# A spectral filter and a snake MLP on one core: the w_in load, batch 1's x loads, its first and inverse pieces and a negation are moved

## The chip, the core and the metric

The kernel runs on one core of one Trainium2 chip. The metric is device time in microseconds of a whole execution; lower is better. Three executions of the kernel before gave 787.63, 787.67 and 788.89 us, a median of 787.67.

## What is computed

```python
x: 8 x 3008 x 256 f32; filt_r, filt_i: 1505 x 256; w_in: 256 x 2048; w_out: 2048 x 256; alpha: 2048
X = rfft(x, axis=1)                       # over the 3008 tokens, per channel
y = irfft(X * (filt_r + 1j*filt_i))       # a circular filter, per channel
h = y.reshape(24064, 256) @ w_in
g = h + sin(alpha*h)**2 / alpha           # "snake"
out = g @ w_out                           # 24064 x 256 f32
```

## The kernel before, in words

**The filter.** The transform of 3008 = 47 x 64 points is done with matmuls in f16 in four kinds of piece, for each batch b, in class Spectral. *first* (L178, matmul L181, result pa): the DFT over 47, 16 pieces of 94x512; four of them fill a quarter of t_h, which SP stores to DRAM (d<-t_h, L186). *load_t2* (L193): eight DMAs issued by POOL bring that back transposed (t<-d); all of them read every quarter. *forward* (L201, result pb): the DFT over 64 with its twiddles, 12 pieces; ACT evacuates pb to xf (L204), and SP swaps xf's halves into xs with two DMAs (L208). *product* (L215) and *cross* (L221, L222) multiply by the filter on DVE, the cross with xs. *inverse* (L232, result pc), 12 pieces; three of them fill g, which SP stores (d<-g, L239). *load_t4* (L244) reads that back (t_a<-d), and *last* (L254, result pd), 16 pieces, gives y, with channels on partitions. Evacuations of pa, pc and pd go through `evac` (L160 on ACT, L162 on DVE), every third on DVE by a counter that runs over the program. pa, pb, pc and pd of all batches share two PSUM buffers (pool fps).

Batch 0 has a way of its own without DRAM: transposes on DVE (L413), matmuls L399, L431, L453, products L441, and L343 for the last step, whose later parts are put between other matmuls one by one ("between").

**The MLP.** 48 chunks of up to 512 columns of y. *hidden* (L540, ph, two matmuls of 512 columns; cos on ACT, L544; L545 on DVE makes v), 16 per chunk, with four PSUM buffers. *project* (L557, po, eight matmuls of 256 columns; copy to o, L565; stores, L585, half a dozen small DMAs on SP for 256 rows).

**Start-up.** POOL's queue loads x of batch 0, the table d_t, the filter and the table e_t. The filter comes in four quarters (L303), two halves g of the frequencies, real (k = 0) and imaginary (k = 1), each in two DMAs; `marks["filt", g, k]` is the second DMA of a quarter. The first of SP's six w_in loads (L468) waits for one of these marks; SP's queue is in order, so the other w_in loads, two small tables (L471, L472) and the two halves of w_out (L475) come after it. weights_in (L482) multiplies w_in by alpha on POOL, in six products, the first after batch 0's last filter product; weights_out (L514) multiplies w_out by -0.5/alpha on POOL in three, and on ACT (L512) for the last four blocks. Between these products POOL issues batch 1's four x loads (L141), of which each needs w_out's first half to have landed. w_out's buffer is the one that v of chunk 1 takes.

**The order.** It is written by hand: a chunk has 8 steps, and each step records two hidden, then what is due, then project, then what is due half a step later (loop at the end). `put(at, ...)` gives a piece its due step; `slot` takes pieces that are due in that order, but only one PE piece at a time unless the next is more than a step late. Each engine executes its instructions in the order recorded. For batch 1: first at 7.9 + 0.3 i, load_t2 at 12.5, inverse at 23.5 + 1.25 u, forward 6 steps before its inverse, product half a step and cross four steps after forward. negate (L602) turns the sign of one half of the imaginary filter, after batch 0 is done with it, in two instructions on DVE at 13 and 14.

The lines most used below are 141, 160, 162, 181, 193, 201, 204, 208, 221, 222, 232, 239, 244, 254, 343, 468, 482, 514, 540, 544, 545, 557, 565, 585 and 602.

Of the kernel before, what the change touches and what calls it, by code (L numbers as in the profile page):

```python
# [62 lines left out]
def kernel(  # L63
# [10 lines left out]
    nc = tc.nc  # L74
# [12 lines left out]
    def after(ins, other):  # L87

        tc.add_manual_dep(ins.ins, other.ins.name, mybir.DependencyInfo(
            mybir.DependencyClass.Sync, mybir.DependencyReason.DATA), reason="order of loads")  # L90
# [43 lines left out]
    f_t = [filt_t[:, k] for k in range(2)]  # L134

    marks = {}
# [150 lines left out]
    def spread_alpha(i):  # L287

        ps = hps.tile([128, 4, 128], FP32, name=f"al_bc_{i}", tag="h")
        for a in range(4):  # L290
            for k, part in enumerate(parts):
                nc.tensor.matmul(out=ps[:, a, :], lhsT=one[:, 4 * i + a:4 * i + a + 1].to_broadcast([128, 128]),
                                 rhs=part, start=(k == 0), stop=(k == 2))
        nc.scalar.copy(out=alpha[:, i // 2, 512 * (i % 2):512 * (i % 2) + 512], in_=ps.rearrange("p a b -> p (a b)"))

    for g in range(2):
        gs = slice(12 * g, 12 * g + 12)
        for k, filt in enumerate((filt_r, filt_i)):
            for q in range(2):
                if (g, k, q) == (0, 1, 1):  # L300
                    split_alpha()
                off, step = ((12 * g) * C, C) if q == 0 else ((N1 - 12 * g) * C, -C)
                marks["filt", g, k] = nc.gpsimd.dma_start(  # L303
                    out=f_t[k][64 * k + 32 * q:64 * k + 32 * q + 32, gs, :],
# [158 lines left out]
    for g in range(6):  # L463
        own, tag = (t2pool, "t2") if g < 3 else (gpool, "g")
        j0 = 1024 * (g // 3) + 384 * (g % 3)
        js = slice(j0, j0 + (256 if g % 3 == 2 else 384))
        w_in32.append((js, own.tile([128, 2, js.stop - js.start], FP32, name=f"w_in_{g}", tag=tag)))
        ins = nc.sync.dma_start(out=w_in32[g][1], in_=w_in_v[:, :, js])  # L468
        if g == 0:
            after(ins, marks["filt", 1, 1])  # L470
    nc.sync.dma_start(out=wf_t, in_=wf_dram.ap())  # L471
    nc.sync.dma_start(out=wi_t, in_=wi_dram.ap())  # L472
    w_out32 = vpool.tile([128, 16, C], FP32, name="w_out32", tag="v")
    for jb in range(0, 16, 8):
        ins = nc.sync.dma_start(out=w_out32[:, jb:jb + 8],  # L475
                                in_=moe_w_out[128 * jb:128 * jb + 1024].rearrange("(b p) c -> p b c", p=128))
        marks.setdefault("w_out", ins)
    s1 = Spectral(1)
# [37 lines left out]

    spread_alpha(2)
    spread_alpha(3)
    for step in ([(weights_in, g) for g in range(6)] + [(s1.load_x, 0), (weights_out, 0), (s1.load_x, 1),
                 (weights_out, 4), (s1.load_x, 2), (weights_out, 8), (s1.load_x, 3)]):  # L520
        step[0](*step[1:])
    warm_pe(12)
    last_0(0, 4)
# [69 lines left out]
    def put(at, fn, *args, pe=False):  # L593
        pending.append((at, len(pending), pe, fn, args))
# [4 lines left out]
    def negate(i):  # L599

        gs = slice(12 * i, 12 * i + 12)
        nc.vector.tensor_scalar(out=f_t[1][0:64, gs, :], in0=f_t[1][0:64, gs, :],  # L602
                                scalar1=-1.0, scalar2=None, op0=ALU.mult)

    for i in range(2):
        put(13 + i, negate, i)
    for n0, n, at in ((6, 5, 1.5), (11, 4, 12.5), (15, 4, 14), (19, 4, 15.5), (23, 4, 17), (27, 5, 19)):
        put(at, last_0, n0, n, fps, "f", True)
    for b in range(1, B):
        s = s1 if b == 1 else Spectral(b)  # L610
        z = 48 * b
        if b > 1:
            for ch in range(4):
                put((22,27,32,37)[ch] if b == 2 else z - 92 + 7 * ch, s.load_x, ch)
        for i in range(16):
            put(7.9 + 0.3 * i if b == 1 else 36 + 0.66 * i if b == 2 else z - 67 + 0.66 * i, s.first, i, pe=True)
        for g in range(4):
            put(12.5 if b == 1 else max(z - 56, 46.5), s.load_t2, g)
        for u in range(12):
            inv = 23.5 + 1.25 * u if b == 1 else 59 + 2.1 * u if b == 2 else z - 40.8 + 2.3 * u  # L620
            fwd = inv - (6 if b == 1 else 6)
            put(fwd, s.forward, u, pe=True)
            put(fwd + (0.5 if b == 1 else 1.5), s.product, u)
            if s.fused:
                put(fwd + (4 if b == 1 else 4.5), s.cross, u)
            put(inv, s.inverse, u, pe=True)
        for ch in range(4):
            put(z - (9.5 if b == 1 and ch < 3 else (10.5, 10.5, 10.5, 3)[ch]), s.load_t4, ch)
        for u in range(16):
            put(z + (u - (5 if b == 1 else 6.5) if u < 4 else 2 * u - 9), s.last, u, pe=True)  # L630
# [15 lines left out]
    step = 0  # L646
# [43 lines left out]
```

## Time and profile before

| | us |
|---|---|
| median of three runs | 787.67 |
| span of the profiled execution, first to last instruction | 786.7 |
| PE busy from 36 to 48 (of 12 us) | 11.28 |
| 48 to 64 (16) | 14.55 |
| 64 to 72 (8) | 6.76 |
| 72 to 80 (8) | 7.81 |
| 80 to 100 (20) | 20.00 |
| 100 to 118 (18) | 17.12 |
| 118 to 135 (17) | 16.96 |
| 135 to 200 (65) | 64.87 |

The profile is of one execution. No time of its own is listed for it beside its span; the span is 1.0 us under the median of the runs, which also holds what lies before the first instruction and after the last. Busy time of PE counts a matmul until its modelled end, and matmuls are pipelined, so a stretch that is busy throughout can still hold waits: what PE loses is better read from the starts of its matmuls. The granted clock is full in all 40 slices of the span. In the lines quoted below, "0.67 <-ACT t_h L160" at the end of a line is the idle time of the engine before it and what ended that; "x4" is the number of instructions merged; a matmul's own 0.38 us is its latency, not its share of the engine's time.

### The profile page before, as it was taken

How to read it: one execution, taken by the hardware profiler on the slowest of the kernel's cores; microseconds unless marked ns; L12 is line 12 of the kernel's file. 1: busy time of each engine (PE TensorE's matmuls, PEld its weight loads, DVE VectorE, ACT ScalarE, POOL GpSimd, SP SyncE). 2: the span in 40 equal slices, each digit the busy share in tenths (PEclk: the TensorE clock that was granted, in tenths of full speed). 3: DMA queues.
4: the chain of work that ended last, by engine and by line, in shares of the span. 5: the costliest groups of instructions: out<-in, count | busy, mean ns of one | idle time of the engine just before them, and what ended most of it. 6: DMA issues, size and time to landing. Idle time of an engine off the chain costs nothing.

```text
span 786.7 us, 16619 instructions
## 1 busy us (share of the span) xinstructions
PE 773.5 (98%) x5799; PEld 535.0 (68%) x5799; DVE 657.6 (84%) x1172; ACT 616.5 (78%) x1208; POOL 79.5 (10%) x125
## 2 busy tenths in 40 slices
PE   8998999999999999999999999999999999999998
PEld 4756766666667766777666766777666776766666
DVE  7887997899878997799977998799987999777773
ACT  5797878888878887888877888788887887777674
POOL 6442000200020000200020000200002000000000
PEclk9999999999999999999999999999999999999999
DMA  9965568665473646554575454845556243421111
GB/s 213 258 131 157 113 145 223 153 123 133 134 198 84 134 99 195 143 120 110 120 200 128 103 106 139 224 87 113 129 155 181 61 99 81 117 62 28 41 41 54
DMA packets 87692, 100.99 MB, mean 128 GB/s; under 512 B 14488, under 2 KB 75944, under 8 KB 87608
## 3 DMA queue, kind: packets, MB, share of 16 engines
q1 hardware_dynamic: 78032, 73.73, 34.5%
q0 software_dynamic: 9360, 26.15, 17.7%
q8 instruction: 45, 0.74, 0.4%
q14 instruction: 39, 0.32, 0.1%
q10 hardware_dynamic: 216, 0.05, 0.0%
HBM read 55.72 MB, written 46.66 MB: 130 GB/s over the span
## 4 chain that ended last, share of the span: by engine, by line
PE 89%; DVE 5%; ACT 2%; DMA 2%; issue 1%; SPq 1%; ACTq 0%; DVEq 0%
PE po L557 39%; PE ph L540 38%; PE pa L181 3%; PE pd L254 2%; DVE v L545 2%; PE pb L201 2%; PE pc L232 2%; DMA xs<-xf 1%; ACT cos_all L544 1%; DMA al<-in_moe_alpha_dram 1%; PE warm L381 1%; PE pc L453 0%; SPq L585 0%; ACT t_h L160 0%; DVE filt_t L162 0%
## 5 line engine op out<-in xcount | busy, mean ns | idle before, releaser
L545 DVE SCALAR_TENSOR_TENSOR v<-cos_all,ph 128x512 f16<-128x512 f32 (+1 forms) x768 | 483.0, 672 | 108.1 <-ACT cos_all L544 104.8
L544 ACT ACTIVATE cos_all<-ph 128x512 f32<-128x512 f32 (+1 forms) x768 | 411.1, 592 | 93.9 <-PE ph L540 92.9
L540 PE MATMUL ph<-y,w 128*128 128x512 f16 (+1 forms) x1536 | 388.4, 374 | 1.7 <-DVE y L162 0.9
L557 PE MATMUL po<-w,v 128*128 128x256 f16 x3008 | 389.5, 272 | 0.0
L557 PEld LDWEIGHTS <-v 128*128 128x128 f16 x3008 | 288.3, 98 | 77.7 <-issue 1.4
L540 PEld LDWEIGHTS <-w 128*128 128x128 f16 x1536 | 147.9, 98 | 106.5 <-issue 6.1
L565 ACT COPY o<-po 128x512 f32<-128x512 f32 (+1 forms) x97 | 55.6, 574 | 20.2 <-PE po L557 12.9
L204 ACT CAST xf<-pb 128x512 f16<-128x512 f32 x84 | 50.0, 595 | 16.4 <-PE pb L201 12.7
L193 POOL DMA_DIRECT2D t<-d x56 | 36.4, 669 | 204.6 <-DMA out_dram<-o 99.8
L160 ACT CAST t_h<-pa 96x512 f16<-96x512 f32 x74 | 43.3, 585 | 10.6 <-PE pa L181 10.5
L141 POOL DMA_DIRECT2D x<-in_x_dram x32 | 17.1, 536 | 298.2 <-PE pc L232 171.2
L160 ACT CAST y<-pd 128x376 f16<-128x376 f32 (+1 forms) x82 | 39.5, 482 | 8.8 <-PE pd L254 5.3
L254 PEld LDWEIGHTS <-t_a 96*128 96x128 f16 x448 | 31.3, 97 | 18.7 <-issue 0.4
L181 PE MATMUL pa<-x,wf_t 94*96 94x512 f16 x112 | 42.3, 381 | 1.6 <-ACT t_h L160 1.3
L160 ACT CAST g<-pc 128x512 f16<-128x512 f32 x58 | 34.4, 593 | 8.0 <-PE pc L232 7.7
L222 DVE TENSOR_TENSOR p<-p,xs 128x512 f16<-128x512 f16 x84 | 35.7, 425 | 2.9
L254 PE MATMUL pd<-wi_t,t_a 96*128 96x94 f16 x448 | 37.1, 204 | 0.0
L221 DVE TENSOR_TENSOR xs<-xs,filt_t 128x512 f16<-128x512 f16 x84 | 35.2, 420 | 0.8 <-DMA xs<-xf 0.8
L215 DVE TENSOR_TENSOR p<-xf,filt_t 128x512 f16<-128x512 f16 x84 | 35.2, 419 | 0.0
L232 PE MATMUL pc<-p,e_t 128*128 128x256 f16 x168 | 32.1, 273 | 0.8 <-ACT xf L204 0.5
L201 PE MATMUL pb<-t,d_t 128*128 128x256 f16 x168 | 32.1, 272 | 0.2
L162 DVE CAST y<-pd 128x376 f16<-128x376 f32 (+2 forms) x46 | 24.9, 544 | 1.5 <-PE pd L343 1.0
(66 smaller groups left out, 264.4 us busy)
## 6 DMA issues: line engine op xcount, KB each, us to landing
x<-in_x_dram POOLq DMA_DIRECT2D x30, 376.0 KB, 4.9
d<-t_h SPq DMA_DIRECT2D x28, 384.0 KB
t<-d POOLq DMA_DIRECT2D x56, 192.0 KB, 4.6
xs<-xf SPq DMA_DIRECT2D x168, 64.0 KB
d<-g SPq DMA_DIRECT2D x56, 192.0 KB
t_a<-d SPq DMA_DIRECT2D x28, 384.0 KB
out_dram<-o SPq DMA_DIRECT2D x104, 80.0 KB
w_out<-in_moe_w_out_dram SPq DMA_DIRECT2D x2, 1024.0 KB
```

The source lines that it names most:

```text
L160: marks["act"] = nc.scalar.copy(out=dst, in_=src)
L181: marks["pe"] = nc.tensor.matmul(out=ps[0:NK, :], lhsT=wf_t, rhs=self.x[ch][:, 2 * j:2 * j + 2, :], start=True, stop=True)
L193: nc.gpsimd.dma_start(out=self.t2[g][64 * p:64 * p + 64, :, :], in_=self.d1[a0:a0 + 6, :, :].rearrange("s n c -> n s c"))
L201: nc.tensor.matmul(out=ps[:, i, :], lhsT=d_t[:, s, :], rhs=self.t2[s // 6][:, s % 6, :], start=True, stop=True)
L204: nc.scalar.copy(out=self.xf[u], in_=ps)
L232: nc.tensor.matmul(out=ps[:, i, :], lhsT=e_t[:, 2 * w + i, :], rhs=pt[:, i, :], start=(k == 0), stop=(k == len(pr) - 1))
L254: nc.tensor.matmul(out=psv[:, i, :], rhs=wi_t, start=True, stop=True, lhsT=t4_h[ch // 2][0:NK, n0 % 16 + i, cb * 128:cb * 128 + 128])
L540: nc.tensor.matmul(out=ps[:, 0:n], lhsT=w1[:, cb, jb * 128:jb * 128 + 128], rhs=y_cols[:, cb, c0:c0 + n], start=(cb == 0), stop=(cb == 1))
L544: nc.scalar.activation(out=cs[:, 0:n], in_=ps[:, 0:n], func=AFT.Sin, bias=float(np.pi / 2))
L545: marks["snake"] = nc.vector.scalar_tensor_tensor(out=v[k][:, jb, 0:n], in0=cs[:, 0:n], scalar=-1.0, in1=ps[:, 0:n], op0=ALU.add, op1=ALU. ...
L557: nc.tensor.matmul(out=pso[k][:, t % 2, :], lhsT=v[k][:, jb, 128 * t:128 * t + 128], rhs=w2[:, jb, :], start=(jb == 0), stop=(jb == 15))
L565: nc.scalar.copy(out=o[:, i0:t % 2 + 1, :], in_=pso[k][:, i0:t % 2 + 1, :])
```

## The change

w_in's first load waits for the second half's real quarter, the third of four, in place of its imaginary quarter, the last. POOL issues batch 1's x loads between the last w_in products, and all w_out products come after them. The two negations run on POOL, at 8 and 9. Batch 1's first pieces are due at 6.9 + 0.37 i and its inverse pieces at 22 + 1.4 u, and forward, product and cross keep their distances from these. One line is added, so that lines after 520 have a number one higher in the changed kernel.

```diff
         ins = nc.sync.dma_start(out=w_in32[g][1], in_=w_in_v[:, :, js])
         if g == 0:
-            after(ins, marks["filt", 1, 1])
+            after(ins, marks["filt", 1, 0])
...
-    for step in ([(weights_in, g) for g in range(6)] + [(s1.load_x, 0), (weights_out, 0), (s1.load_x, 1),
-                 (weights_out, 4), (s1.load_x, 2), (weights_out, 8), (s1.load_x, 3)]):
+    for step in ([(weights_in, g) for g in range(3)] + [(s1.load_x, 0), (weights_in, 3), (s1.load_x, 1),
+                 (weights_in, 4), (s1.load_x, 2), (weights_in, 5), (s1.load_x, 3)]
+                 + [(weights_out, jb) for jb in (0, 4, 8)]):
         step[0](*step[1:])
...
     def negate(i):
 
         gs = slice(12 * i, 12 * i + 12)
-        nc.vector.tensor_scalar(out=f_t[1][0:64, gs, :], in0=f_t[1][0:64, gs, :],
+        nc.gpsimd.tensor_scalar(out=f_t[1][0:64, gs, :], in0=f_t[1][0:64, gs, :],
                                 scalar1=-1.0, scalar2=None, op0=ALU.mult)
 
     for i in range(2):
-        put(13 + i, negate, i)
+        put(8 + i, negate, i)
...
-            put(7.9 + 0.3 * i if b == 1 else 36 + 0.66 * i if b == 2 else z - 67 + 0.66 * i, s.first, i, pe=True)
+            put(6.9 + 0.37 * i if b == 1 else 36 + 0.66 * i if b == 2 else z - 67 + 0.66 * i, s.first, i, pe=True)
...
-            inv = 23.5 + 1.25 * u if b == 1 else 59 + 2.1 * u if b == 2 else z - 40.8 + 2.3 * u
+            inv = 22 + 1.4 * u if b == 1 else 59 + 2.1 * u if b == 2 else z - 40.8 + 2.3 * u
```

## The prediction

> **What bounds the kernel now.** I read the engines' busy time and the 40 slices first, then the waits of PE from 36 to 135 us, then PE's timeline there, and at each wait the timeline of the engine that ended it.
>
> ```profile
> PE 773.5 (98%) x5799; PEld 535.0 (68%) x5799; DVE 657.6 (84%) x1172; ACT 616.5 (78%) x1208; POOL 79.5 (10%) x125
> PE   8998999999999999999999999999999999999998
> ```
>
> ```profile
> PE pa L181 <- ACT t_h L160: 1.3, 2, 0.7
> PE ph L540 <- DVE y L162: 0.9, 1, 0.9
> PE ph L540 <- DVE v L545: 0.6, 1, 0.6
> PE pc L232 <- ACT xf L204: 0.5, 1, 0.5
> ```
>
> TensorE is the bound; after about 135 us it never waits for long, so a saving or a loss before that reaches the end whole. A ph pair costs 0.43 us of issue, a po block of 8 costs 0.87, a pa, pb or pc 0.22, a pd matmul 0.04 (differences of starts in PE's timeline). What the starts show beyond that is lost time. In batch 1's first pieces and what follows:
>
> ```profile
> 62.51 0.38 PE L181 MATMUL pa<-x,wf_t 94*96 94x512 f16 x1 [0.67 <-ACT t_h L160]
> ...
> 68.69 0.38 PE L540 MATMUL ph<-y,w 128*128 128x512 f16 x1 [0.90 <-DVE y L162]
> ...
> 72.40 0.38 PE L201 MATMUL pb<-t,d_t 128*128 128x256 f16 x2
> ```
>
> pa 15 (62.51) waits for an evacuation, ph of chunk 2 (68.69) for DVE, and pb 0 (72.40) for nothing. From pb 3 (81.10) to pa 3 of batch 2 (117.99) PE issues 34 ph (14.7), 17 po blocks (14.8), 21 pb and pc (4.6) and 3 pa (0.6), 34.7 of 36.9 us: 2.2 us lost. Half of it starts here, in SP's queue and on ACT:
>
> ```profile
> 93.49 1.33 SPq L239 DMA_DIRECT2D d<-g  x2
> 94.93 1.49 SPq L208 DMA_DIRECT2D xs<-xf  x2
> 96.54 3.00 SPq L585 DMA_DIRECT2D out_dram<-o  x7
> ```
>
> ```profile
> 100.66 0.59 ACT L204 CAST xf<-pb 128x512 f16<-128x512 f32 x1 [1.32 <-DMA xs<-xf]
> ...
> 104.88 0.58 ACT L204 CAST xf<-pb 128x512 f16<-128x512 f32 x1 [1.68 <-DMA xs<-xf]
> ```
>
> xs 7 is issued 2.6 us after its xf is there (92.31), since the g store stands ahead of it on SP; it lands at 100.6, ACT's xf 10 waits for that, xs 8 too, and PE (101.30) and DVE are late from then on.
>
> **The change part by part.** All is counted against the profiled span, 786.7 us; the median of the runs is 787.67, 1.0 above it, and I carry the differences over to the median.
>
> *w_in behind the third quarter.* The third quarter lands at 23.0, the fourth at 25.45 (issues at 15.16 and 16.36 plus 7.9 and 9.1 to landing, in the filter tile's view), so the load starts 2.4 us sooner. Nothing waits for w_in: POOL's first product starts at 30.54, as the last batch 0 product ends. What it can cost is the fourth quarter, whose copy (L162, 25.66, the DVE chain that sets the end of the start-up) begins 0.2 us after it lands.
>
> ```profile
> 24.00:25.00 1.00, 1.00 (x16) 1.00 (x14) 0.97 (x2) 1.00 (x3) 0.00 (x0) 1.00 0.63 115
> 25.00:26.00 1.00, 1.00 (x16) 1.00 (x14) 0.97 (x2) 1.00 (x3) 0.00 (x0) 1.00 0.12 40
> 26.00:27.00 1.00, 0.61 (x10) 0.43 (x7) 0.87 (x2) 1.00 (x3) 0.00 (x0) 1.00 0.63 48
> ```
>
> The last columns are DMA share and GB/s. w_in was issued at 25.47 and its second microsecond took 0.63 of the engines. 2.4 us sooner that meets the tail's 0.63: 1.26, so 0.26 too much; less the 0.2 of slack, and bounded by 0 and by a doubled tail (1.0): I take **+0.1**, the near end, since a load's first microsecond is thin (48 GB/s at 26 to 27).
>
> [...] No row here has the two loads at once.
>
> *x between the w_in products.* On POOL three issues of 0.57 us now stand ahead of products 4 to 6, so these end at 37.9, 40.3 and 42.1 instead of 37.3, 39.1 and 40.2; ph 11 needs the fifth at 43.06 and ph 14 the sixth at 45.41: margins of 2.7 and 3.3 us, cost 0. The three w_out products move behind all four issues and end near 48.0 instead of 47.4; DVE needs the buffer of w_out at about 49.2 (below): margin 1.2. The first x issue waits for the first half of w_out, due 2.4 us earlier; even undelayed it would cost 1 us of those margins. x lands about 4.5 us after issue, at 40 to 47, well ahead of its first use in both programs. Value 0; above, 1 us if both margins fail.
>
> *negate on POOL.* DVE loses two instructions of 0.94 us (62.62, 65.58). POOL runs them right after w_out, at 48, and is then idle until 67.10. Their price there is not shown: between 0.94 us each and three times POOL's 1.91 us for 1024 columns (5.7 us for 3072); even 11.5 us ends at 59.5, and the first reader is at about 80. Cost 0. DVE's 0.61 us cadence is the same with POOL busy (38 to 47) and idle (50). What DVE gains is the 0.9 at 68.69: the y evacuation ends at 67.7 instead of 68.64. That is **not** paid out, see the next part.
>
> *First pieces earlier, forward earlier.* pa 0 and pa 1 now precede chunk 1's first ph. pa 2 then waits for pa 0's evacuation, which stands behind two activations on ACT (46.73, 47.22) and ends at 48.27: 0.6 us lost. Walking on with the same durations, two pa to 1.73 us of other work, PE has pa 12 at 58.8 and pa 15 at **62.0**, still behind the evacuation of pa 14; gain 0.5 against 62.51. The last first piece is due at the same place as before (12.45 for 12.4), and pa 15 stands just ahead of ph 12 in both.
>
> But pb 0 moves forward by one po block, one ph pair and another po block with their pd (1.03 + 0.86 + 1.03 = 2.9 us). Its data come by a chain the change leaves as it is: evacuation of pa 15, store, load of t on POOL, landing.
>
> ```profile
> 67.10 5.22 POOL L193 DMA_DIRECT2D t<-d  x8 [19.14 <-DMA d<-t_h]
> ```
>
> Evacuated at 63.51, loads issued from 67.10, the first two landed at 70.54 and 71.34: 7.8 us. Before, PE came at 72.40, 1.06 after it. Now the evacuation ends at 63.0, the data are there at 70.9, and PE arrives at 68.5 (67.7 for the late ph, 0.8 for the rest of the two ph and pd): it waits 2.4 us. pb 0 ends at 71.13, and the 2.9 us that before lay ahead of it follow: 74.05 against 72.62. **+1.4** at equal work, with all gains of the earlier parts inside; ends 0 (the chain 1.4 quicker) and +2.0 (pa 15 no earlier).
>
> *Inverse pieces at 1.4 for 1.25.* The 0.2 at pb 2 (78.19) goes: its predecessor in the buffer is earlier. **-0.25.** In the long stretch each cross now stands 0.2 step ahead of the forward three pieces later, whose xs reuses its buffer; before it stood 0.25 step behind. DVE needs per step 1.19 for two L545 and 1.13 + 0.2 per piece: 2.25 of PE's 2.08 us before, 2.14 of 2.04 now. The g store goes out about 1.4 us earlier relative to PE, so xs 7 is no longer behind it, and pc 6 no longer waits for xf 10's evacuation. Of the 2.2 us I expect 0.6 to stay (pc 10, with its cross at the same place, 0.4); ends 0.2 and 2.2. **-1.6.**
>
> *pc 11* goes behind ph 12 and 13 and its evacuation from ACT to DVE: about 2 us later relative to PE. Behind it are the g store, the t_a load and pd 0 of batch 1, where PE already waits 0.2 (127.77). The t_a load also stands behind another store and an x load, which hide part: **+0.6**, ends 0 and 1.5.
>
> Sum: 0.1 + 1.4 - 0.25 - 1.6 + 0.6 = +0.25: **787.9 us**.
>
> **Rivals.** *Slower: the wait at pb 0 stays and is not earned back.* Its place is the load of t, its price 1.4. It decides if xs still lands late, so that the stretch to 118 keeps its 2.2: 0.1 + 1.4 - 0.25 + 0 + 1.0 = +2.2, 789.9. For it: the store and load chain is untouched, and the stores of out still stand between xs 7 and xs 8. Against: the order on SP does improve. *Faster: t is there when PE comes.* Then the 0.97 at 68.69 counts in full: -1.0 - 0.25 - 1.6 + 0.5 = -2.35, 785.3. For it: the loads meet less traffic if the stores are out earlier; against: 3.5 us for the store and 3.4 for the load were measured with spare DMA. *The w_in part does harm alone:* the fourth quarter doubled, +1.0 on the rest: 788.8. *The change does nothing:* gains and losses cancel, 787.7.
>
> **How the numbers follow.** 0.2% (1.6 us) is about what a measurement of this kernel can tell from no change. Forecast, cancellation and w_in harm, all within it: 0.52. Slower rival 0.27; faster rival 0.21. Range: the ends of pb 0 (0 to 2.0) and of the long stretch (-2.0 to 0) rule; leaving out a tenth on each side, 785.6 to 790.2.
>
> **What would show it.** Right: PE idle for about 2.4 us before pb (L201) near 68.5 to 71, ended by DMA t<-d; pa 15 near 62; no DVE L602 on DVE, POOL with two instructions near 48; ACT's waits on xs gone or below 1 us; a wait at pd (L254) near 127 of about 1 us. Wrong: no wait at pb 0 (faster), waits at pc of over 1.5 us between 100 and 118 (slower), the copy of the fourth quarter later than 26.2 (w_in harm), or a wait of ph for w1.

## The result, and the profile after

The changed kernel took **791.53 us** (median of six executions, 789.59 to 794.03), the kernel before on the same chip 788.46 (six, 787.63 to 788.98): a ratio of 1.004, interval 1.0023 to 1.0058. On a second chip, with 12 executions against 31, it was 791.48 to 789.20, 1.0023 (1.0010 to 1.0035). So it is slower by 0.2 to 0.4%, where 787.9, no change, was forecast, and 791.5 lies above the range of 785.6 to 790.2.

The profiled execution does not show that. Its span is 787.8 us, 1.1 above that of before, its time 789.59, the lowest of its six, and its granted clock full:

```profile
PE 771.4 (98%) x5799; PEld 535.0 (68%) x5799; DVE 655.7 (83%) x1170; ACT 616.4 (78%) x1208; POOL 95.2 (12%) x127
...
PE   7998999999999999999999999999999999999998
...
PEclk9999999999999999999999999999999999999999
```

The waits of PE from 36 to 136 us (total, times, longest) answer to those shown of before:

```profile
PE pb L201 <- DMA t<-d: 2.2, 1, 2.2
PE pd L254 <- DMA t_a<-d: 1.4, 1, 1.4
PE pa L181 <- ACT t_h L160: 1.3, 3, 0.7
PE ph L541 <- DVE y L162: 0.8, 1, 0.8
PE ph L541 <- DVE v L546: 0.6, 1, 0.6
PE pc L232 <- DVE g L162: 0.3, 1, 0.3
```

The two at the top are new, and both wait for a landing. The wait for xf at pc is gone. The timeline of PE has the first pieces' end and the late pb 0 as the prediction placed them:

```profile
61.45 0.38 PE L181 MATMUL pa<-x,wf_t 94*96 94x512 f16 x1 [0.67 <-ACT t_h L160]
...
67.19 0.38 PE L541 MATMUL ph<-y,w 128*128 128x512 f16 x1 [0.83 <-DVE y L162]
...
70.32 0.38 PE L201 MATMUL pb<-t,d_t 128*128 128x256 f16 x2 [2.20 <-DMA t<-d]
```

ACT from 70 to 120 us no longer waits for xs; its waits, in full:

```profile
ACT cos_all L545 <- PE ph L541: 5.8, 8, 0.9
ACT xf L204 <- PE pb L201: 1.8, 2, 1.6
ACT g L160 <- PE pc L232: 1.4, 3, 0.7
ACT t_h L160 <- PE pa L181: 1.1, 2, 0.6
ACT y L160 <- PE pd L343: 0.4, 1, 0.4
```

And POOL's timeline (start, duration):

```profile
37.41 0.58 POOL L141 DMA_DIRECT2D x<-in_x_dram  x1 [2.54 <-PE ph L541]
...
44.51 5.59 POOL L514 TENSOR_TENSOR w<-w_out,rec_t 128x1024 f16<-128x1024 f32 x3
50.09 15.90 POOL L603 TENSOR_SCALAR filt_t<-filt_t 64x3072 f16<-64x3072 f16 x2
66.04 4.64 POOL L193 DMA_DIRECT2D t<-d  x7
```

The first x issue stood still for 2.54 us. The line names PE as what ended that. In the program this issue waits for w_out's first half, whose landing the profile does not list; in e3 below w_out's load is issued 2.36 us later and this x issue comes 1.81 later, so w_out is the likelier cause. The w_out products end at 50.1, and each negation took 7.95 us where DVE takes 0.94. They end 0.05 us before the t load goes out. That is luck, not a cause: 3.57 us lie between the issue of the last d store and the t load here (62.47, 66.04) as in before (63.53, 67.10), and in e5, the same kernel again, POOL stands idle for 1.81 us between the negations and the t load.

What PE loses beyond its issue cost, summed from its starts as in the prediction, in the two profiled executions:

| us of the span | before | after | difference | forecast |
|---|---|---|---|---|
| 0 to 40, start-up | 10.66 | 10.19 | -0.47 | +0.1 |
| 40 to 80, first pieces and pb 0 | 6.45 | 7.58 | +1.13 | +1.15 |
| 80 to 120, the long stretch | 2.28 | 1.32 | -0.96 | -1.6 |
| 120 to 140, pd 0 of batch 1 | 0.62 | 2.02 | +1.40 | +0.6 |
| sum | | | +1.10 | +0.25 |

That accounts for the 1.1 us of this execution. It leaves the rest, and the spans with their clocks point to it: 787.8 (1.000), 792.3, 789.6, 788.8, 789.8 (all 0.998) and 791.2 (0.995). In most executions TensorE's mean granted clock was lower.

### The profile page after: what moved, and what is told of

The parts are those of the page before. It is cut to its first block, busy times and chain, and to the rows that moved or that the text cites. A ratio compares the mean times of both kernels' runs of the same rounds, so it can differ in the third digit from the quotient of the medians.

```text
span 787.8 us, 16616 instructions
## 1 busy us (share of the span) xinstructions
PE 771.4 (98%) x5799; PEld 535.0 (68%) x5799; DVE 655.7 (83%) x1170; ACT 616.4 (78%) x1208; POOL 95.2 (12%) x127
## 4 chain that ended last, share of the span: by engine, by line
PE 88%; DVE 5%; DMA 2%; ACT 2%; issue 1%; SPq 0%; POOL 0%; ACTq 0%; POOLq 0%
PE po L558 39%; PE ph L541 38%; DVE v L546 3%; PE pa L181 3%; PE pd L254 2%; PE pc L232 2%; PE pb L201 2%; ACT cos_all L545 1%; PE pc L453 1%; DMA al<-in_moe_alpha_dram 1%; ACT t_h L160 1%; PE warm L381 1%; DMA t_a<-d 1%; PE pb L431 1%; DMA t<-d 0%
```

## The experiments

Of the experiments, e1, e2, e3 and e6 to e8 are edits of the changed kernel, and e5 is that kernel itself; e9, e10 and e11 start from e8, and e4 and e12 from the kernel before. *Full-clock span* is the mean over executions of span times mean clock: what is left if the share of TensorE's clock that was not granted is taken out (clocks are listed to 0.001, about 0.8 us of a single span). It takes out somewhat too much, since it also counts clock that was not granted while TensorE had nothing to do: in e5's profile the granted clock is 0.50 from 69.45 us, and PE stands idle until 70.98. At the end of the program the clock falls too: in the profiles of before and of the changed kernel it is 0.50 from 787.96 and 789.25 us, just behind the span (786.7, 787.8), after 3.41 us without work. PE's last matmul ends some 3.65 us before the span does in both (783.07 and 784.16), so in an execution whose grid lies otherwise (e5 below) such a fall can come within the span; this is an estimate from these times. So a listed 0.999 need not mean a loss, and what follows from this column for the clock is an upper estimate. The ratios are those on record; they differ by up to 0.001 from the quotients of the medians listed.

| kernel | executions | median us | ratio to before (interval) | mean span | mean clock | full-clock span |
|---|---|---|---|---|---|---|
| before, beside e1 to e4 | 24 | 789.32 | | 787.68 | 0.9995 | 787.26 |
| before, beside e5 to e8 | 31 | 789.20 | | 787.60 | 0.9995 | 787.24 |
| before, beside e9 to e12 | 33 | 789.27 | | 787.64 | 0.9995 | 787.26 |
| e5, changed kernel | 12 | 791.48 | 1.0023 (1.0010-1.0035) | 789.49 | 0.9978 | 787.71 |
| e1, inverse as before | 12 | 787.62 | 0.9976 (0.9968-0.9985) | 785.85 | 0.9998 | 785.72 |
| e2, both waits filled | 12 | 790.61 | 1.0017 (1.0007-1.0027) | 789.07 | 0.9994 | 788.61 |
| e3, w_in as before | 6 | 795.19 | 1.0069 (1.0043-1.0094) | 793.28 | 0.9962 | 790.24 |
| e4, before + inverse | 7 | 792.25 | 1.0034 (1.0021-1.0046) | 790.41 | 0.9979 | 788.72 |
| e6, half filled | 12 | 789.70 | 1.0010 (0.9997-1.0023) | 788.47 | 0.9996 | 788.14 |
| e7, pb 0 late | 12 | 787.59 | 0.9978 (0.9967-0.9989) | 786.06 | 0.9998 | 785.86 |
| e8, pb 0 and pc 11 late | 8 | 787.05 | 0.9963 (0.9949-0.9977) | 785.27 | 0.9996 | 784.98 |
| e9, e8 + negate on DVE | 11 | 786.69 | 0.9972 (0.9962-0.9983) | 785.32 | 0.9995 | 784.89 |
| e10, e8 + first as before | 11 | 788.28 | 0.9986 (0.9976-0.9997) | 786.36 | 0.9999 | 786.29 |
| e11, e8 + w_in, x as before | 11 | 786.65 | 0.9971 (0.9962-0.9980) | 785.12 | 0.9995 | 784.69 |
| e12, before + w_in early | 11 | 788.34 | 0.9991 (0.9982-0.9999) | 786.57 | 0.9999 | 786.50 |

### Which part does it, and is it the clock?

**e1: inverse and forward pieces back.**

```diff
-            inv = 22 + 1.4 * u if b == 1 else ...
+            inv = 23.5 + 1.25 * u if b == 1 else ...
```

> The changed kernel with batch 1's inverse pieces back at 23.5 + 1.25u (so the forward pieces back at 17.5 + 1.25u); the rest of the change stays. Theory 'clock': in the profiled run the change costs only 1.1 us of span, and what the other runs are longer (spans 788.8 to 792.3 at a clock of 0.995 to 0.998, against 787.8 at 1.000) is TensorE at a lowered clock after its new idle stretches (2.2 us ahead of pb 0, 1.4 us ahead of pd 0 of batch 1). Here pb 0 comes one and a half steps later, after its data: no wait over 0.5 us there nor at pd 0, clock 1.000 in every run, span 786 to 787, median 787 to 788.5. Rival 'elsewhere': the lowered clock comes from what the change does at the start-up (w_in, x, negate); then most runs still show 0.995 to 0.998 and the median is 789 to 791.

All clocks were 0.999 or 1.000, the median 787.62, the profiled span 785.5. The wait at pb 0 was gone, 0.3 us were left at pd 0. The loss is in this one line; the rest of the change makes the kernel 0.24% faster.

**e4: that line alone, on the kernel before.**

```diff
-            inv = 23.5 + 1.25 * u if b == 1 else ...
+            inv = 22 + 1.4 * u if b == 1 else ...
```

> The kernel before with only batch 1's inverse pieces at 22 + 1.4u (forward pieces at 16 + 1.4u); w_in, x, negate and the first pieces as before. Theory 'clock': pb 0 stands 1.5 steps earlier while its t lands at 70.5 to 71.3 as before, so PE waits 1.5 to 2.5 us there and 1 to 1.5 at pd 0; most runs at 0.995 to 0.998, median 790 to 792. Rival 'elsewhere': the start-up is that of before, so clock 1.000, and the median within 1 us of the kernel before.

792.25, a little above what the theory gave; the profiled execution waits 1.75 us at pb 0 and 1.52 at pd 0, and all seven clocks are 0.997 or 0.998. Its profile caught a lowered clock. Cut at the moments at which the clock record changes (columns: stretch; its length; busy time and count of PE, PEld, DVE, ACT, POOL; **granted clock**; DMA share; GB/s):

```profile
64.66:68.07 3.41, 2.54 (x24) 2.07 (x22) 3.35 (x6) 2.15 (x5) 1.23 (x2) 1.00 0.19 64
68.07:71.49 3.42, 1.30 (x10) 0.96 (x10) 1.69 (x3) 1.53 (x3) 3.42 (x7) 1.00 0.86 236
71.49:74.90 3.41, 3.41 (x17) 2.00 (x15) 0.88 (x2) 1.18 (x2) 0.56 (x1) 0.50 1.00 271
74.90:78.31 3.41, 3.28 (x31) 2.78 (x30) 1.92 (x3) 2.68 (x6) 0.00 (x0) 1.00 0.35 79
```

The stretch before the fall holds the wait: PE was busy 1.30 of 3.41 us. The whole next stretch runs at 0.50, with 17 matmuls in it where the one after it has 31.

**e2: the two waits filled with work that nothing reads.** Matmuls go into pb 0's and pd 0's own buffers, ahead of the real ones.

```diff
+    def keep_busy(ps, n):
+        for _ in range(n):
+            nc.tensor.matmul(out=ps, lhsT=d_t[:, 0, :], rhs=e_t[:, 0:4, :], start=True, stop=True)
...
+            if (b, u) == (1, 0):
+                keep_busy(ps.rearrange("p a c -> p (a c)"), 10)   # 6 ahead of pd 0
```

> The changed kernel with 10 matmuls of 512 columns that nothing reads put into pb 0's own buffer just ahead of its real ones, and 6 into that of pd 0 of batch 1 (2.1 and 1.3 us of work, in the place of 2.2 and 1.4 us of waiting; the real matmuls still wait for the same landings). Theory 'clock': clock 1.000 in every run, spans within 0.5 us of the profiled 787.8, median 789 to 790, that is 1.5 to 2.5 less than the changed kernel for MORE work on TensorE. Rival 'elsewhere': runs at 0.995 to 0.998 as before and a median of 791 to 792. Rival 'plain waiting' (the waits are simply longer in the other runs, and the clock figure is only their shadow): the same 791 to 792, with a longer wait left ahead of pb 0 or pd 0.

Half right. Ten of 12 executions were at 0.999 or 1.000, and no wait was left at either place in the profile. But two were at 0.998, and the full-clock span rose to 788.61: the filling was priced at nothing, and it cost 0.9 us at a full clock against the changed kernel in e5 (1.35 and 0.47 us over the kernel before, each on its own chip). The time does not show the theory cleanly; that of e6 below does.

**e3: w_in behind the fourth quarter again.**

```diff
-            after(ins, marks["filt", 1, 0])
+            after(ins, marks["filt", 1, 1])
```

> The changed kernel with the w_in load held behind the fourth filter quarter again, as before; the rest of the change stays. Theory 'clock': the waits at pb 0 and pd 0 stay, so median 790.5 to 792.5 with most runs at 0.995 to 0.998; the w_in load alone is worth less than 0.5 us either way. Rival 'w_in': the early load disturbs the start-up; then this gives back 2 us or more, 788 to 789.5, clock 1.000.

Theory and rival were both wrong: 795.19, worse than either. In its profile w_out's load is issued at 29.19 for 26.83 and the first x issue on POOL, which stands ahead of w_in products now, at 39.22 for 37.41; a pa then waits 0.8 us at 49.34, pb 0 2.4 at 72.27 and pd 0 1.8 at 135.69. With the new order on POOL the late w_in delays what stands behind it. The clock fell to 0.50 from 71.42 to 78.24, two stretches of 3.41 us, after one with 1.07 us busy.

### How long must the idle time be?

**e5: the changed kernel again, without an edit.**

> The changed kernel itself, beside the next three on one chip. In the two profiles that caught a lowered clock the granted clock changes on a grid of 3.413 us, and falls to 0.50 for the windows that follow one in which TensorE was idle for 2.12 and 2.34 us; windows with 1.84 us idle or less are followed by 1.00. Theory 'clock by window': here the two idle stretches of the changed kernel (66.4 to 67.2 and 68.1 to 70.3) put over 2 us into one window for some two thirds of the phases the grid can have; so over half of the runs at 0.998 or less, others at 1.000, 0.2 to 0.6% over the kernel before. Rival 'noise of the first measurement': all at 1.000, within 0.2%.

Nine of 12 executions were at 0.998 or less, three at 1.000; 1.0023 to before. The profile caught a lowered clock. First the slices of the page, then the stretches, cut as above:

```profile
PEclk9998999999999999999999999999999999999999
```

```profile
66.04:69.45 3.41, 1.34 (x10) 0.85 (x9) 2.04 (x4) 2.12 (x4) 3.32 (x6) 1.00 0.51 153
69.45:72.86 3.41, 1.88 (x11) 1.47 (x12) 0.48 (x1) 0.59 (x1) 1.98 (x4) 0.50 1.01 268
72.86:76.28 3.42, 3.42 (x16) 1.95 (x15) 1.89 (x4) 1.20 (x2) 0.00 (x0) 0.50 0.75 159
76.28:79.69 3.41, 3.28 (x28) 2.53 (x26) 1.54 (x4) 2.07 (x4) 0.00 (x0) 1.00 0.11 25
```

One digit 8 in the fourth slice of the page is all that it shows; at half the clock four ph matmuls take 1.91 us (73.38) for 1.03 in the first profile of this kernel (71.58). That first profile, cut on its own grid:

```profile
65.63:69.04 3.41, 1.67 (x14) 1.17 (x12) 1.95 (x4) 2.35 (x5) 3.36 (x6) 1.00 0.42 138
69.04:72.45 3.41, 2.13 (x19) 1.61 (x20) 1.36 (x3) 0.92 (x3) 2.28 (x4) 1.00 0.93 251
```

The same kernel and the same two waits, here from 66.4 to 67.2 and from 68.1 to 70.3; but here a border of the grid, at 69.04, cuts the long one in two, and neither half is idle enough. (In e5 the long one lasts 2.78 us instead of 2.20. Of the 2.8 us by which its profiled span is longer, 0.6 are therefore plain waiting. The window that lowered the clock ended at 69.45, before that made a difference.) The grid, with borders 3.413 us apart, has one at 6.31 us in before, at 4.19 in the first profile of the changed kernel, at 4.60 in e5 and at 6.56 in e3 (the last two counted back from the stretches printed), so its phase differs from one execution to the next. In the windows read (all of before and of the changed kernel's first profile, and those printed of e3, e4 and e5), from the first border on and while TensorE had work left, the full clock fell after windows that were busy for 1.07 (e3), 1.30 (e4) and 1.34 us (e5) (idle 2.34, 2.12, 2.07), and not after 1.56 (idle 1.84, in e3 at pd 0, shown here with the window behind it) or 1.67 (idle 1.75, the changed kernel's first profile).

```profile
132.86:136.27 3.41, 1.56 (x16) 1.08 (x15) 1.22 (x3) 1.52 (x4) 0.00 (x0) 1.00 0.97 257
136.27:139.69 3.42, 3.42 (x30) 2.58 (x29) 2.02 (x5) 2.69 (x6) 0.00 (x0) 1.00 0.91 286
```

The windows at the end of the program agree: the clock fell after one with nothing busy (784.55 to 787.96 in before, 785.84 to 789.25 in the first profile of the changed kernel), and not after one with 1.94 us busy (781.13 to 784.55) or 1.74 (782.43 to 785.84). A window already at 0.50 is another matter: 2.56 us busy, 0.85 idle, was followed by 0.50 again (e3, from 71.42). For the two idle stretches of the changed kernel two thirds of all phases (0.67, an estimate worked out from those times) put over 2.07 us into one window, and 0.81 of them over 1.84; 14 of its 18 executions had 0.998 or less. In e5 2.07 us in one window, in two gaps of 0.82 and 1.25, were enough.

**e6: five matmuls ahead of pb 0, none ahead of pd 0** (the edit of e2 with 5 for 10).

> The changed kernel with 5 matmuls of 512 columns that nothing reads ahead of pb 0, in its own buffer: 1.1 us of the 2.2 us wait are filled, 1.1 stay, and so does the 1.4 at pd 0. Theory 'clock by window': no window holds 2 us of idle time any more, so every run at 1.000 or 0.999 and the median 1 to 2 us below that of the changed kernel in the same call, although the landing that pb 0 waits for is no earlier and TensorE has more to do. Rival 'plain waiting': the same median as the changed kernel, within 0.5 us.

```profile
PE pd L261 <- DMA t_a<-d: 1.1, 1, 1.1
PE pb L208 <- DMA t<-d: 1.1, 1, 1.1
```

These are its waits (seven lines lower in the file). Every clock was 0.999 or 1.000, and the median 789.70 against 791.48, 1.8 us less, with more work on PE and no earlier landing. No window can now hold more than 1.9 us of these idle times (0.8 and 1.1). Mean spans: 1.0 us less, made of 1.4 gained by the clock and 0.4 more at a full clock, which is about the scatter of such a difference. So the idle time cost beyond its own length here, and keeping PE busy through half of the wait at pb 0 took that part away.

### What the waits themselves are worth

**e7: only pb 0 and pb 1 back.**

```diff
             fwd = inv - (6 if b == 1 else 6)
+            if b == 1 and u < 2:
+                fwd = 17.5 + 0.4 * u
```

> The changed kernel with only forward pieces 0 and 1 of batch 1 put back to 17.5 and 17.9 (before: 17.5 and 18.75); all other pieces stay at the 1.4 spacing. The wait at pb 0 goes (below 0.3 us), the one at pd 0 stays (1.2 to 1.6). Theory 'clock by window': every run at 1.000 or 0.999; the profiled span falls by about the 2.2 us of the wait to 785.3 to 786.3, and the median by 3 to 4 us against the changed kernel in the same call. Rival 'pd 0 does it too': runs at 0.998 remain, and the median falls by 2.2 or less.

3.9 us off the median, as the theory had it. Mean span 3.4 less: 1.85 at a full clock, the rest clock. The wait at pd 0 stays:

```profile
PE pd L254 <- DMA t_a<-d: 1.6, 1, 1.6
PE pa L181 <- ACT t_h L160: 1.3, 3, 0.7
```

and 11 of 12 clocks are 0.999 or 1.000 (one is 0.998). So pd 0's wait by itself lowers the clock seldom if at all: its 1.6 us are below the 2.07, and no second gap stands beside it.

**e8: and pc 11 back**, on top of e7.

```diff
+            if b == 1 and u == 11:
+                inv = 37.25
```

> As the last, and inverse piece 11 of batch 1 put back to 37.25 (the changed kernel has 37.4), which puts it ahead of the pieces of batch 2 that passed it. The wait at pd 0 falls from 1.4 to 0.3 us. Both theories: the span 1 us below the last kernel's, 784.3 to 785.3, clock 1.000. Against the kernel with all inverse pieces back (span 785.5, 0.24% below the kernel before) it keeps the 1.4 spacing between, which in the profiles takes 0.7 to 1.0 us off the waits of pc from 90 to 118: 0.3 to 0.45% below the kernel before. Rival 'the spacing brings nothing': the same as that kernel within 0.3 us.

The wait at pd 0 is gone; all that is left of PE's waits from 36 to 136 us:

```profile
PE pa L181 <- ACT t_h L160: 1.3, 3, 0.7
PE ph L541 <- DVE y L162: 0.8, 1, 0.8
PE ph L541 <- DVE v L546: 0.6, 1, 0.6
PE pc L232 <- DVE p L222: 0.2, 1, 0.2
```

0.9 us less again at a full clock; 787.05, by the ratio 0.37% under the kernel before (0.23 to 0.51%), by the medians 0.27%. It can't be told apart from e9 and e11 below. Against e1, on another chip, the 1.4 spacing is worth 0.7 us at a full clock, of which 0.3 is the wait that e1 still has at pd 0.

### The other parts, undone one by one on e8

**e9: negations on DVE at 13 + i.**

```diff
-        nc.gpsimd.tensor_scalar(out=f_t[1][0:64, gs, :], in0=f_t[1][0:64, gs, :],
+        nc.vector.tensor_scalar(out=f_t[1][0:64, gs, :], in0=f_t[1][0:64, gs, :],
...
-        put(8 + i, negate, i)
+        put(13 + i, negate, i)
```

> The kernel with both pieces put back late (e8_both_late), and with the two negations on DVE again at 13 + i. By the prediction's step, DVE's y evacuation ends 0.9 us later and nothing now covers it, since pb 0 no longer waits: the wait of ph ahead of pb 0 grows from 0.8 to about 1.7 us, span 785.2 to 785.6, median 0.7 to 1.1 above e8_both_late in its call relative to the kernel before (ratio 0.9972 to 0.9978 against 0.9963). The t load can then go out as soon as the last d store has landed, not at the end of the negations. Rival: the negations on POOL were worth nothing (ratio within 0.0005 of 0.9963).

The ratio, 0.9972, lies on the near edge of the forecast, but its interval overlaps e8's, and the step forecast is not there: the profiled span is 784.5, as in e8, where 785.2 to 785.6 was expected, and the full-clock spans are 784.89 and 784.98. The gain of 0.9 is not found. In DVE's timeline

```profile
64.70 0.94 DVE L603 TENSOR_SCALAR filt_t<-filt_t 64x3072 f16<-64x3072 f16 x1
65.56 0.53 DVE L162 CAST y<-pd 128x376 f16<-128x376 f32 x1
66.02 1.27 DVE L546 SCALAR_TENSOR_TENSOR v<-cos_all,ph 128x512 f16<-128x512 f32 x2
67.22 0.54 DVE L162 CAST y<-pd 128x376 f16<-128x376 f32 x1
```

the negation delays the first y, but ph then waits 0.89 us, against 0.83 with it on POOL, where about 1.7 was expected (a wait of pd for ACT of 0.3 us, which before has too, comes back). The second y, for which ph waits, follows right behind a v in both: in the changed kernel PE issues its last pd at 66.16, and DVE copies it from 66.59 to 67.13, behind a v that began at 65.99. What of the wait is the order on DVE and what the way of pd itself stays open; the negation makes no difference to it.

**e10: first pieces at 7.9 + 0.3 i.**

```diff
-            put(6.9 + 0.37 * i if b == 1 else ...
+            put(7.9 + 0.3 * i if b == 1 else ...
```

> e8_both_late with batch 1's first pieces at 7.9 + 0.3i as before. By the prediction's step the wait at pa 2 (0.6) goes and a wait of 0.8 at pa comes back near 59, the y evacuation and t come up to 0.5 us later relative to the work; the pieces themselves are worth 0.5 us: ratio 0.9965 to 0.9972. Rival: they were the gain of the change, 1.0 us or more (ratio 0.9975 or above).

The rival was right: 1.3 us at a full clock. The earlier first pieces are the largest gain found in the change, and part of it pays a debt of the new order on POOL. DVE's v of chunk 1 takes w_out's buffer and now waits for the w_out products:

```profile
49.67 1.28 DVE L546 SCALAR_TENSOR_TENSOR v<-cos_all,ph 128x512 f16<-128x512 f32 x2 [1.43 <-POOL w L514]
50.88 0.68 DVE L162 CAST t_h<-pa 96x512 f16<-96x512 f32 x1
```

With the pieces at their old place, pa waits 0.88 us at 51.61 for that evacuation; with the new one DVE's wait is 1.39 us too, and PE has none there.

**e11: the head of the program as before** (w_in behind the fourth quarter; all w_in products, then x and w_out in turn).

> e8_both_late with the w_in load behind the fourth quarter and the old order on POOL (all w_in products, then x and w_out in turn). By the prediction these two are worth 0.1 or less: ratio 0.996 to 0.9968. Rival 'coupled': x of batch 1 now lands as late as before (44.6 to 51.8) for first pieces that come one step earlier, and the negations start 1 us later on POOL and hold the t load; waits of pa for x, 1 us or more: ratio 0.9975 or above.

0.9971 to 0.9963, between what was forecast and the rival: no difference that the intervals show, and the full-clock spans are 784.69 and 784.98. In its profile no pa waits for x. So x as late as before does no harm on this base, and the rival falls; on the changed kernel itself e3 showed that the late w_in alone, under the new order on POOL, does.

**e12: w_in early alone, on the kernel before** (the first hunk of the change).

> The kernel before with only the w_in load held behind the third quarter. By the prediction +0.1 us (ends 0 to 1.0): ratio 1.000 to 1.0005. [...] Rival 'gain': w_in and w_out arrive 2.4 us earlier and something used that: ratio 0.999 or below.

0.9991 (0.9982 to 0.9999): a gain of 0.7 us, where e11 shows none on another base. The fourth quarter's time from issue to landing did not grow: 9.1 us in before, 9.0 in the changed kernel with w_in behind the third quarter. So the late fourth quarter, the prediction's rival of harm by w_in, falls. Where the 0.7 comes from stays open.

## Why the prediction was wrong

**The step that failed** is the one at pb 0: "it waits 2.4 us", priced as "**+1.4** at equal work" with ends of 0 and +2.0. The wait was there, at the place named, for the reason named and of the size named (2.2 us of idle time before 70.32). What it cost was not its length alone: together with the 0.8 us for y just ahead of it, which the prediction knew too, it left TensorE idle for 2.07 us of one window of 3.41 us in e5's profile, and for the next two windows the granted clock was 0.50 (in e4's, 2.12 us and one window). The prediction looked at the clock once, saw it full in before, and took durations at that clock for granted. On the second chip the clock is worth 1.4 us of the 1.9 by which the mean spans differ, and the rest, 0.47 us at a full clock, is close to the 0.25 of the sum. Within e5 itself the three executions at 1.000 have a mean span of 788.0 us, the nine others 790.0. e1, e6 and e7 show that it is this wait. By the prediction's own figures the wait made a difference of 2.4 us (+1.4 with it, -1.0 in the rival without it); e7, which takes it away, moved the mean span by 3.4, of which 1.85 at a full clock.

That the sum is so near the 0.47 is partly luck: in the profiled pair the long stretch gained 0.6 less than forecast and pd 0 cost 0.8 more, while the start-up came out 0.6 better, and the standard error of the 0.47 is some 0.3 us.

Point by point:

- *w_in, +0.1*: no harm, as forecast; the copy of the fourth quarter began at 25.16, against 25.66 in before. No run shows the doubled fourth quarter and the +1.0 of the w_in rival: the quarter took 9.0 us from issue to landing, against 9.1 in before. The -0.5 of the profiled start-up is the spread of executions: the stall of ph for v that stands at 44.21 and 43.72 us in the two profiles lies anywhere from 43.55 to 44.69 in those of e5 to e9, which have one and the same start-up.
- *x between the products, 0*: right in sum, as far as e11 can tell. But both margins were misjudged: the first x issue waited 2.54 us, in all likelihood for w_out, and the w_out products, "near 48.0", ended at 50.1, so that DVE waited 1.4 us. PE was spared only by the new place of the first pieces (e10).
- *negate on POOL*: its price, "between 0.94 us each and 5.7", was 7.95 us each. It stayed hidden, since the t load waited for the store until the same moment. The gain of 0.9 for y was not found (e9).
- *First pieces*: pa 2's wait 0.59 us (0.6 forecast), pa 15 at 61.45 (62.0, less the 0.5 of the start-up). The 0.5 us given for the gain was small: 1.3 in e10.
- *Inverse spacing, -1.6*: right in kind, ACT's waits for xs are gone; -0.96 in size.
- *pc 11, +0.6 with ends 0 and 1.5*: +1.4 in the profile and 0.9 in e8 against e7; near the far end. "The t_a load also stands behind another store and an x load, which hide part" did not hold.
- *Rivals*: the slower one named the place, a wait at pb 0 that is not earned back, but gave it a long stretch without gain as the reason. That stretch did gain; the clock took it back.

## What to carry to other kernels

Where TensorE is the bound, don't price a new wait by its length alone: add up all its idle time within any 3.4 us around, the step of the grid here. In these runs 2.07 (e5) and 2.34 us (e3) of it in one window were followed by two windows of 3.41 us at 0.50, 2.12 (e4) by one, and 1.84 (e3, at pd 0) by none; 14 of the changed kernel's 18 executions had a clock of 0.998 or less. A piece moved forward of its own data was a loss, which a later place in the order cured here (1.85 us at a full clock in e7, 0.9 more in e8); work that kept TensorE busy for part of the gap saved the clock in e6 (0.999 or 1.000 in all 12 executions). And read the clocks of all executions listed, not only the profile's: the one with the profile may be one that got away.

## What the runs showed of the hardware

- In these profiles the granted clock changes on a grid of 3.413 us whose phase differs from run to run (borders at 6.31 us in before, 4.19 in the changed kernel's first profile, 4.60 in e5). While TensorE had work left, the full clock fell to 0.50 after windows with 1.07 (e3), 1.30 (e4) and 1.34 us (e5) of PE work, and not after 1.56 (e3). It came back after windows that were busy throughout: windows at half clock with 1.88 (e5) and 2.56 us (e3) busy were followed by another at 0.50, the three with 3.41 or 3.42 (e3, e4, e5) by 1.00. Where between 1.34 and 1.56, and between 2.56 and 3.41, the borders lie is not known.
- POOL's tensor_scalar in place, 64x3072 f16, took 7.95 us (the changed kernel's profile), 8.5 times DVE's 0.94 (before, e9).
- Matmuls put into a gap to hold the clock were not free: ten and six of them (e2) cost about 0.9 us at a full clock, where they were to fill waits of 2.2 and 1.4 us. Five ahead of pb 0 (e6) cost 0.4, which the scatter does not tell from nothing.
